# Second products of a fused convolution and SoLU layer taken one tile later, with a sixth buffer of transposed p

## The chip, the cores and the metric

One core of a Trainium2 chip runs the whole program. The metric is the device time of one execution in microseconds (us). Three timed runs of the kernel before gave 1180.63, 1186.45 and 1187.74 us, a median of 1186.45. The profiled execution took 1186.25 us by the same clock; its profile spans 1184.5 us from the first to the last instruction, and 1.75 us lie around it.

## The reference

The input x has 8 sequences of 4160 rows and 192 columns. A causal convolution of 7 taps runs along each sequence, with one softmaxed set of taps for each of 8 heads of 24 columns. Its 33280 rows go through a SoLU layer:

```
h    = y @ w_in                                  # 192 -> 1024
e    = exp(h - max(h));  sm = e / (sum(e) + 1e-9)
solu = h * sm
ln   = (solu - mean(solu)) / sqrt(var(solu) + 1e-6) * g_ln
out  = ln @ w_out                                # 1024 -> 192
```

Inputs and outputs are float32 (w_in, w_out and g_ln arrive as 64-bit words). The kernel splits each operand of a matmul into an upper and a lower half of 16 bits and adds three products, which keeps nearly all of float32's precision.

## The kernel before, in words

**Tiles and chunks.** A tile is 128 rows; there are 260. The convolution works on chunks: chunk 0 has 1024 rows, chunk 1 has 1056, and chunks 2 to 16 have 2080 each (16.25 tiles). A chunk's x arrives in four pieces (`Chunk.load`, L141 to L169) into eight buffers `xr`, so that a piece of chunk n+2 takes a buffer of chunk n. The peaks of a piece are taken in eight steps by VectorE (`sum_squares`, L183), a small matmul adds them up (`add_up`), a chain of eight small VectorE operations makes the chunk's scales (`scale_steps`, L194 to L213), and the last link of that chain writes three columns of `cv` on GpSimd (L210). Then GpSimd splits each piece into halves in three operations (`halve_steps`, L243, L247, L250); those are put in a queue with costs, and `queue.run(budget)` issues entries as long as its credit is above zero (L1146). TensorE convolves the halves (`fold`, L1654), ScalarE and VectorE write the result as upper and lower y (L320, L329), and three transposing DMAs for each of a chunk's two parts turn y into yT (`turn`, L359).

**One tile.** TensorE makes ph = y @ w_in in two PSUM banks (`up_half`, L802). VectorE takes the row's extreme (`emit_max`, L853), ScalarE the exponential e (`emit_exp`, L860), VectorE the numerators ph times e (`emit_mul`, L870), ScalarE their upper half (`emit_hi`, L881) and the sum of squares (`emit_square`, L885), and GpSimd the lower half (`emit_lo`, L896). The same call then has SyncE (SP) issue one transposing DMA, which turns both halves, p, into pT (L898). TensorE makes the second product po = pT @ w_out (`out_half`, L932), VectorE moves po to a group's buffer (`emit_evac`, L969), and when a group of 8 tiles has its roots (`Group.roots`, GpSimd, L1027 to L1031), each row block is scaled and stored. Four buffers hold e, four hold p16, five hold pT (tag `pT`, taken in turn), three pairs of PSUM banks hold ph or a convolution, and two single banks hold po.

**The order of the work is written out by hand** (`manual_schedule`): each engine, and SP's queue of DMAs too, executes its instructions in the order in which the functions issue them. Tiles 0 to 31 go in pairs and threes, tiles 32 to 253 in 111 calls of `two_steps(i)` (L1693), the last six in `three_steps(254)` and `last_three`. One call of `two_steps` issues for TensorE: the first products of tiles i and i+1 (a and b) but for half of b's; one half of the second products of two earlier tiles, x = i-5 and z = i-4; the rest of b; the other half of x and z. Two tiles share the array, 64 rows each, so x and z run side by side, and both must be there when the first half begins. With s = (tile of b in its chunk) // 2, steps with odd s have two groups of products of the next chunk's convolution placed within the first half of x and z (`fold`), as long as there is a next chunk; the step with s = 1 also has the small matmul of `add_up`.

GpSimd's order within step i is: lower half of tile i-2 (`emit_lo(pa)`), `queue.run(2.0)`, the scales of `cv` if the chain is there, lower half of tile i-1 (`emit_lo(pb)`), a second `queue.run(2.0)`. SP's order is: stores, a load of x, the transpose of tile i-2, turns of y, the transpose of tile i-1. Second products of a step therefore use a tile whose `emit_lo` was issued late two steps before (i-5) and one whose `emit_lo` was issued early in the step before (i-4).

```
        x, z = tiles[i - 5], tiles[i - 4]
...
        up_half(a, sa, 1)
...
            out_half(x, z, 0)
```

Of the kernel before, what the change touches and what calls it, by code (L numbers as in the profile page):

```python
# [8 lines left out]
F16 = mybir.dt.float16  # L9
F32 = mybir.dt.float32  # L10
# [10 lines left out]
def kernel(  # L21
# [10 lines left out]
    P = 128  # L32
    B, S, D = x.shape
    H, K = weight.shape
# [3 lines left out]
    NFC = F // P  # L38
    NH = F // 512
    HALO = 16  # L40
    CW = P - HALO
    NB = 2 * D // P
    NT = B * S // P
# [25 lines left out]
    cp = ctx.enter_context(tc.tile_pool(name="cp", bufs=1))  # L69
    xp = ctx.enter_context(tc.tile_pool(name="xp", bufs=1))  # L70
    yp = ctx.enter_context(tc.tile_pool(name="yp", bufs=2))
    sp = ctx.enter_context(tc.tile_pool(name="sp", bufs=3))
# [11 lines left out]
    def single(name):  # L84

        nonlocal singles
        singles += 1
        return ps.tile([P, 512], F32, name=name, tag=f"single{singles % 2}")
# [333 lines left out]
        compare_op=ALU.is_equal, fill=0.0, base=0, channel_multiplier=1,  # L422
    )
    NS = CW - TB
    shift = cp.tile([P, NS + P], F16, name="shift")
    pool.memset(shift, 1.0)
    pool.affine_select(
        out=shift, in_=shift, pattern=[[1, NS + P]],
# [130 lines left out]
    valued(halves[0], dve)  # L559


    taps = cp.tile([P, H, CW], F32, name="taps")
    taps_hi = cp.tile([P, H, CW], F16, name="taps_hi")
    taps_lo = cp.tile([P, H, CW], F16, name="taps_lo")
    NQ = CW // TB
# [9 lines left out]
    for e, bank in enumerate(banks):  # L575
        for q in range(2 * per):
            j = q // 2
# [109 lines left out]
        nc.sync.dma_start(wlo[low, 1, :], wlo[top, 1, :])  # L687


    o_inv = cp.tile([P, 1], F32, name="o_inv")  # L690
    t_out = cp.tile([P, 1], F32, name="t_out")
    osq = cp.tile([P, 1], F32, name="osq")
    wof = wo.f.rearrange("p (c d) -> p c d", d=D)
    mean = None
    out_halves = [slice(0, NFC * D // 2), slice(NFC * D // 2, NFC * D)]
# [198 lines left out]

    def emit_lo(t, eng):
        eng.tensor_tensor(t.p16[:, :, 1, :], t.halves, t.p16[:, :, 0, :], ALU.subtract)  # L896
        t.pT = sp.tile([P, 2 * NFC, P], F16, name=f"pT_{t.i}", tag="pT", bufs=5)
        nc.sync.dma_start_transpose(t.pT, t.p16.rearrange("p n a f -> p (n a f)"))  # L898

    def emit_halves(t, eng):  # L900
# [14 lines left out]
    def emit_out(t):  # L915
        t.po = single(f"po_{t.i}")
        t.wide = t.grp.n > 1 and t.i >= PAIRED

        ops, per = [], NFC // NH
        for c in range(NFC):  # L920
            hi = c // per * 2 * per + c % per
            if t.wide:
                ops.append((hi, ohl[:, c].rearrange("p a d -> p (a d)"), 2 * D))
            else:
                ops += [(hi, ohi[:, c], D), (hi, olo[:, c], D)]
            ops.append((hi + per, ohi[:, c], D))
        for j, (a, w, n) in enumerate(ops):
            nc.tensor.matmul(  # L928
                t.po[:, 0:n], t.pT[:, a, :], w, start=j == 0, stop=j == len(ops) - 1
            )  # L930
# [32 lines left out]
    def emit_evac(t):  # L963
        if t.grp.raw is None:
            t.grp.open()
        if not t.wide:
            dve.tensor_copy(t.grp.raw[:, t.g, :], t.po[:, 0:D])
        else:
            dve.tensor_reduce(  # L969
                t.grp.raw[:, t.g, :],  # L970
                t.po[:, 0 : 2 * D].rearrange("p (a d) -> p d a", a=2), AX.X, ALU.add,
            )
        (rows if t.grp.ready else t.grp.waiting).append((t.grp, t.g))
# [88 lines left out]
    tiles, lefts, left = [], [], 0  # L1062
    for ch in range(NCH):
        lefts.append(left)
        n = (left + spans[ch][2]) // P
        for k in range(n):
            t = Tile()
# [93 lines left out]
    queue, groups, chain, rooted, rows, stores = Queue(), {}, [], [], [], []  # L1161
# [31 lines left out]
    def run_stores():  # L1193
        while stores:
            stores.pop(0)()

    def run_chain(n):
        while chain and n > 0 and chain[0][1] is None:
            chain.pop(0)[0]()
            n -= 1  # L1200
# [16 lines left out]
    PAIRED = FIRST // P  # L1217
# [4 lines left out]
    def prepare(i):  # L1222
        t = tiles[i]
        c = chunks[t.ch]
        t.yT, t.y2 = c.yT, c.y2
        t.cv = c.cvm if t.k == 0 else c.cv
        pos, n, t.g = t.slot
        if pos not in groups:
            groups[pos] = Group(pos, n)
        t.grp = groups[pos]  # L1230
        return t
# [156 lines left out]
    def others(ts):  # L1388

        work = {}  # L1390
        for q in ts:
            for what, items in chores(q.ch, q.k, q.n).items():
                work.setdefault(what, []).extend(items)
        return work
# [6 lines left out]
    def span(i):  # L1401

        late = i >= 26
        return i - DEPTH + (not late) + (i in (PAIRED, 26)), i - DEPTH + 3 + (not late)

    def three_steps(i):


        a, b, c = ts = [prepare(i + j) for j in range(3)]
        done = [tiles[j] for j in range(*span(i))]  # L1410
        if i == NT - 6:
            leave_two()
            done[0] = None
        work = others(ts)
        added = work.get("sum", [])
        added = [added[:1], added[1:]]
# [24 lines left out]
        def place(n):  # L1441
            for f in [f for f, m in zip(todo, places) if m == n]:
                got.setdefault(n, []).append(f())
            if n == 2 * start:
                total_up(at(n)[0][0].bank if at(n) else None)
# [50 lines left out]
            turns()  # L1496
        run_stores()
        swap = i in (17,20,23,26,)
        if not swap and done[0]:
            emit_out(done[0])  # L1500

        fresh = i == 2 * FIRST // P - 2
# [8 lines left out]
        rest = emit_a(a, b, c, between, not fresh, fresh, behind_rows)  # L1511
        if not behind_rows:
            emit_rows(b, False, True)
        if done[0]:
            emit_evac(done[0])
        place(1)
        run_rows(i)
        uppers(0)
# [174 lines left out]
    def two_steps(i):  # L1693


        a, b = prepare(i), prepare(i + 1)
        x, z = tiles[i - 5], tiles[i - 4]
        ch, s = b.ch, b.k // 2
        c1, c3 = (chunks[ch + j] if ch + j < NCH else None for j in (1, 3))

        run_stores()
        if c3 and s in (0, 1, 2, 4):
            c3.load((0, 1, 2, 4).index(s))
        evacs = []
        if left_over:
            pa, pb, *evacs = left_over
            emit_exp(pb)
        else:
            emit_out(tiles[i - 6])
            evacs = [tiles[i - 6]]  # L1710
            pa = pb = None
        for d in evacs:
            emit_evac(d)
        if pb:
            emit_mul(pb)

        got, summed = [], False
        sa, sb, sc = ring
        up_half(a, sa, 0)
        up_half(b, sb, 0)  # L1720
        up_half(a, sa, 1)
        if s % 2 and c1:
            j = s - 1
            got, half, bank = fold(c1, c1.groups()[j : j + 2], sc)
            out_half(x, z, 0, slice(0, NFC // 2))
            half(0)
            out_half(x, z, 0, slice(NFC // 2, NFC))
            half(1)
            if chain and chain[0][1] is not None and chain[0][1] <= i + 2:
                add_up(i + 2, bank)  # L1730
                summed = True
            ring[:] = [sa, sc, sb]
        else:
            out_half(x, z, 0)
            ring[:] = [sc, sa, sb]
        up_half(b, sb, 1)
        out_half(x, z, 1)

        def move():
            for f in moves[:1]:  # L1740
                f()
            del moves[:1]

        if pa:
            emit_square(pa)
            emit_hi(pb)
            emit_lo(pa, pool)
        else:
            for q in squares:
                emit_square(q)  # L1750
            squares.clear()
        for k, q in doubles:
            k.double(*q)
        doubles.clear()
        move()
        emit_max(a)
        emit_exp(a)
        queue.run(2.0)
        for _ in range(2 + (len(rows) > 8)):
            if rows:  # L1760
                g, j = rows.pop(0)
                g.row(j, act if j % 2 else dve)
        if not summed:
            run_chain(4)
        if c3 and s:
            for j in ((), (0,), (1,), (2,), (3,), (4,), (5, 6), (7,), ())[s]:
                sum_up(c3, c3.halves(j // 2)[j % 2], i)
        for k, pc, hg in got[:1]:
            k.upper(pc, *hg)
        emit_mul(a)  # L1770
        for k, pc, hg in got[1:]:
            k.upper(pc, *hg)
        for k, pc, hg in got:
            k.lower(pc, *hg)
        if pb:
            emit_square(pb)
            emit_lo(pb, pool)
        move()
        emit_hi(a)
        emit_max(b)  # L1780
        run_chain(4)
        queue.run(2.0)
        if got and s in (3, 7):
            part = c1.parts[s == 7]
            if s == 3:
                c1.open(lefts[c1.ch], chunks[ch])
            moves.extend(
                lambda blk=blk: c1.turn(blk, *part) for blk in (1, 0, 2)
            )
            moves.append(lambda: doubles.append((c1, part)))  # L1790
        take_rooted()
        left_over[:] = [a, b, x, z]

    def leave_two():

        a, b, *done = left_over
        run_stores()
        emit_exp(b)
        for d in done:
            emit_evac(d)  # L1800
        emit_mul(b)
        emit_square(a)
        emit_hi(b)
        emit_lo(a, pool)
        emit_lo(b, pool)
        squares.append(b)
# [61 lines left out]
    for i in range(PAIRED, 4 * PAIRED, 3):  # L1868
        three_steps(i)
# [31 lines left out]
```

## Time and profile before

| | |
|---|---|
| median of three runs | 1186.45 us |
| profiled execution, its own time | 1186.25 us |
| its span, first to last instruction | 1184.5 us |
| TensorE matmul busy, weight loads busy | 1130.1 us (95%), 887.3 us (75%) |
| VectorE, ScalarE, GpSimd busy | 992.2 (84%), 998.7 (84%), 891.9 us (75%) |
| DMA | 227.75 MB, 192 GB/s over the span |
| mean granted TensorE clock | 0.994 of full |

The five engines run side by side, each in its own order. Busy shares are means over the span; a short wait of one engine shows in a view of a single stretch. A matmul's end is modelled, since matmuls overlap in the array, so that a TensorE called busy may still be slower than its best pace. In a row of windows the engines' busy times stand in the order PE (TensorE), PEld (its weight loads), DVE (VectorE), ACT (ScalarE), POOL (GpSimd).

### The profile page before, as it was taken

How to read it: one execution, taken by the hardware profiler on the slowest of the kernel's cores; microseconds unless marked ns; L12 is line 12 of the kernel's file. 1: busy time of each engine (PE TensorE's matmuls, PEld its weight loads, DVE VectorE, ACT ScalarE, POOL GpSimd, SP SyncE). 2: the span in 40 equal slices, each digit the busy share in tenths (PEclk: the TensorE clock that was granted, in tenths of full speed). 3: DMA queues.
4: the chain of work that ended last, by engine and by line, in shares of the span. 5: the costliest groups of instructions: out<-in, count | busy, mean ns of one | idle time of the engine just before them, and what ended most of it. 6: DMA issues, size and time to landing. Idle time of an engine off the chain costs nothing.

```text
span 1184.5 us, 34794 instructions
## 1 busy us (share of the span) xinstructions
PE 1130.1 (95%) x13681; PEld 887.3 (75%) x13681; DVE 992.2 (84%) x2024; ACT 998.7 (84%) x1789; POOL 891.9 (75%) x711
## 2 busy tenths in 40 slices
PE   5999998999999999999999999999899999999998
PEld 3675666887869788787877877787687886888866
DVE  7988896887888888888888888888788888788886
ACT  7888996887878888888888888888788788888895
POOL 2867897967779697787868959688596878855664
PEclk9999999999999999999999999999999999999999
DMA  7999999999999999999999999999999999999998
GB/s 205 192 180 190 205 213 213 182 200 191 187 188 209 200 199 193 204 196 206 204 186 194 194 203 185 202 193 178 203 188 200 184 190 163 184 184 177 179 164 180
DMA packets 727474, 227.75 MB, mean 192 GB/s; under 512 B 651647, under 2 KB 725903, under 8 KB 727311
## 3 DMA queue, kind: packets, MB, share of 16 engines
q1 hardware_dynamic: 727310, 225.53, 103.8%
q8 instruction: 108, 1.77, 0.6%
q14 instruction: 56, 0.45, 0.1%
HBM read 33.00 MB, written 25.56 MB: 49 GB/s over the span
## 4 chain that ended last, share of the span: by engine, by line
PE 33%; issue 17%; POOL 12%; DMA 11%; ACT 11%; DVE 9%; PEld 6%; SPq 1%; DVEq 0%; ACTq 0%; POOLq 0%; PEldq 0%
PE po L800 13%; PE ph L800 11%; DMA pT<-p 10%; POOL p L896 7%; PEld L800 6%; DVE ph L853 5%; PE pc L800 3%; ACT sq L885 3%; PE po L928 2%; PE ph L753 2%; ACT e L860 2%; ACT y L320 2%; ACT p L881 2%; DVE e L870 1%; POOL xs L250 1%
## 5 line engine op out<-in xcount | busy, mean ns | idle before, releaser
L896 POOL TENSOR_TENSOR p<-e,p 128x1024 f16<-128x1024 f32 x257 | 547.4, 2134 | 137.6 <-ACT p L881 135.3
L800 PE MATMUL po<-ohl,pT 64*128 64x384 f16 (+1 forms) x7104 | 520.4, 283 | 26.4 <-DMA pT<-p 24.3
L800 PEld LDWEIGHTS <-pT 64*128 64x128 f16 x7104 | 436.2, 94 | 84.8 <-DMA pT<-p 44.4
L800 PE MATMUL ph<-whi,yT 64*128 64x512 f16 x2664 | 487.0, 377 | 4.6 <-DVE e L870 4.0
L870 DVE SCALAR_TENSOR_TENSOR e<-ph,cv,e 128x1024 f32<-128x1024 f32 x248 | 317.9, 1282 | 109.3 <-ACT e L860 108.9
L860 ACT ACTIVATE e<-ph,sm 128x1024 f32<-128x1024 f32 x260 | 289.4, 1113 | 88.6 <-DVE ph L853 75.8
L800 PEld LDWEIGHTS <-yT 64*128 64x128 f16 x3774 | 277.0, 94 | 110.5 <-DVE e L870 4.3
L853 DVE TENSOR_SCALAR_CACHE_REDUCE ph<-ph,cv 128x1024 f32<-128x1024 f32 x248 | 318.9, 1287 | 10.0 <-PE ph L800 7.3
L800 PE MATMUL ph<-wlo,yT 64*128 64x512 f16 x1110 | 300.7, 377 | 0.0
L881 ACT CAST p<-e 128x1024 f16<-128x1024 f32 x245 | 255.8, 1044 | 45.9 <-DVE e L870 45.6
L885 ACT ACTIVATE sq<-e 128x1024 f32<-128x1024 f32 x260 | 273.2, 1051 | 0.2
L969 DVE TENSOR_REDUCE raw<-po 128x192 f32<-128x384 f32 x247 | 126.9, 551 | 5.9 <-PE po L800 3.7
L250 POOL TENSOR_TENSOR xs<-xr,xs 128x960 f16<-128x960 f32 (+1 forms) x56 | 107.4, 1918 | 1.2
L329 DVE SCALAR_TENSOR_TENSOR y<-pc,y 112x432 f16<-112x432 f32 (+5 forms) x140 | 67.8, 532 | 27.3 <-ACT y L320 26.2
L800 PE MATMUL ph<-wlo,y 64*128 64x512 f16 x222 | 83.7, 377 | 0.0
L928 PE MATMUL po<-ohl,pT 128*128 128x384 f16 (+1 forms) x712 | 80.2, 269 | 3.1 <-DMA pT<-p 1.6
L800 PE MATMUL pc<-xs,taps_hi 64*112 64x240 f16 (+1 forms) x832 | 80.8, 259 | 0.0
L928 PEld LDWEIGHTS <-pT 128*128 128x128 f16 x712 | 61.8, 98 | 22.6 <-issue 4.3
L320 ACT ACTIVATE y<-pc 112x432 f16<-112x432 f32 (+5 forms) x140 | 57.1, 470 | 24.1 <-PE pc L800 20.7
L183 DVE TENSOR_REDUCE xa<-xr 128x1 f32<-128x384 f32 x112 | 67.8, 620 | 6.7 <-DMA xr<-in_x_dram 6.7
L800 PE MATMUL pc<-xs,taps_lo 64*112 64x240 f16 (+1 forms) x416 | 70.5, 259 | 0.0
L800 PEld LDWEIGHTS <-taps_hi 64*112 64x112 f16 x832 | 65.6, 128 | 2.2 <-issue 1.7
(166 smaller groups left out, 993.5 us busy)
## 6 DMA issues: line engine op xcount, KB each, us to landing
out_dram<-raw SPq DMA_DIRECT2D x127, 192.0 KB, 2.8
xr<-in_x_dram SPq DMA_DIRECT2D x41, 480.0 KB, 4.7
xr<-in_x_dram SPq DMA_DIRECT2D x22, 384.0 KB, 4.1
pT<-p SPq DMA_TRANSPOSE x263, 5.0
y<-yT SPq DMA_DIRECT2D x15, 140.0 KB, 3.1
y<-yT SPq DMA_DIRECT2D x15, 126.0 KB, 2.8
yT<-y SPq DMA_TRANSPOSE x102, 3.7
raw_out<-in_moe_w_out_dram SPq DMA_DIRECT2D x1, 1536.0 KB, 12.6
```

The source lines that it names most:

```text
L183: dve.tensor_reduce(self.part[:, col : col + 1], self.raw[j][:, a:z, :], AX.XY, ALU.max, apply_absolute_value=True,)
L250: (2.1 * size + 0.2, lambda: pool.tensor_tensor(xl, r, h, ALU.subtract)),
L320: act.activation(self.at(0, col + e, col + z, a, b), pc[:, :, e:z], AF.Copy, scale=self.scale(),)
L800: nc.tensor.matmul(o, lhs, w, start=start, stop=stop)
L853: dve.tensor_scalar(t.ph, t.ph, t.cv[:, 0:1], None, ALU.mult, ALU.min, accum_out=t.bias)
L860: act.activation(t.e, t.ph, AF.Exp, bias=t.bias, scale=-1.0, accum_out=grp.z[:, g : g + 1])
L870: dve.scalar_tensor_tensor(t.e, t.ph, t.cv[:, 3:4], t.e, ALU.mult, ALU.mult, accum_out=t.grp.s1[:, t.g : t.g + 1],)
L881: act.copy(t.p16[:, :, 0, :], t.halves)
L885: act.activation(junk, t.e, AF.Square, accum_out=t.grp.s2[:, t.g : t.g + 1])
L896: eng.tensor_tensor(t.p16[:, :, 1, :], t.halves, t.p16[:, :, 0, :], ALU.subtract)
L928: nc.tensor.matmul(t.po[:, 0:n], t.pT[:, a, :], w, start=j == 0, stop=j == len(ops) - 1)
L969: dve.tensor_reduce(t.grp.raw[:, t.g, :], t.po[:, 0 : 2 * D].rearrange("p (a d) -> p d a", a=2), AX.X, ALU.add,)
```

## The change

- `two_steps` takes the second products of x = i-6 and z = i-5, one tile later than before. At the first such step (i = 32) the separate second product of tile 26 falls away, and at the end `three_steps(254)` makes that of tile 248, which it left out before.
- A sixth buffer of pT, `sixth`, takes every sixth tile from 37 on; the other five go on in turn. It lies where `taps` and `shift` lay, which serve the convolution of the first chunks and are now views of it. `o_inv`, `t_out` and `osq` become columns of one tile.
- The first of the two places in a step where the chain of a chunk's scales goes on issues three links in place of four, so that the GpSimd link (L210) comes at the second place, behind `emit_lo(pb)`.
- The queue is run three times a step with a budget of 1.3 in place of twice with 2.0; the new place is just behind `emit_lo(pb)`.
- While chunk 3 is under way (steps 32 to 46), chunk 6's four pieces of x are loaded at s = 2, 3, 5, 6 in place of 0, 1, 2, 4, and the eight peaks are taken from s = 3 on in place of s = 1. Later chunks keep their places.

```diff
-    shift = cp.tile([P, NS + P], F16, name="shift")
+    sixth = cp.tile([P, 2 * NFC, P], F16, name="sixth")
+    spare = sixth.rearrange("p a b -> p (a b)")
+    shift = spare[:, 2 * H * CW : 2 * H * CW + NS + P]
...
-    taps = cp.tile([P, H, CW], F32, name="taps")
+    taps = spare[:, 0 : 2 * H * CW].bitcast(F32).rearrange("p (h c) -> p h c", h=H)
...
-        t.pT = sp.tile([P, 2 * NFC, P], F16, name=f"pT_{t.i}", tag="pT", bufs=5)
+        if 4 * PAIRED <= t.i < NT - 6 and (t.i - 4 * PAIRED) % 6 == 5:
+            t.pT = sixth
+        else:
+            t.pT = sp.tile([P, 2 * NFC, P], F16, name=f"pT_{t.i}", tag="pT", bufs=5)
...
             leave_two()
-            done[0] = None
...
-        x, z = tiles[i - 5], tiles[i - 4]
+        x, z = tiles[i - 6], tiles[i - 5]
...
-        if c3 and s in (0, 1, 2, 4):
-            c3.load((0, 1, 2, 4).index(s))
+        first = ch == 3
+        when = (2, 3, 5, 6) if first else (0, 1, 2, 4)
+        if c3 and s in when:
+            c3.load(when.index(s))
...
-            emit_out(tiles[i - 6])
-            evacs = [tiles[i - 6]]
...
-        queue.run(2.0)
+        queue.run(1.3)
...
-            run_chain(4)
-        if c3 and s:
-            for j in ((), (0,), (1,), (2,), (3,), (4,), (5, 6), (7,), ())[s]:
+            run_chain(3)
+        if c3:
+            for j in (
+                ((), (), (), (0, 1), (2,), (3,), (4, 5), (6, 7)) if first
+                else ((), (0,), (1,), (2,), (3,), (4,), (5, 6), (7,), ())
+            )[s]:
...
             emit_lo(pb, pool)
+            queue.run(1.3)
...
         run_chain(4)
-        queue.run(2.0)
+        queue.run(1.3)
```

## Rows read from the trace of the kernel before

**Rows 1.** Page, part 1: busy time (share) and instructions of each engine.
```profile
PE 1130.1 (95%) x13681; PEld 887.3 (75%) x13681; DVE 992.2 (84%) x2024; ACT 998.7 (84%) x1789; POOL 891.9 (75%) x711
```

**Rows 2.** TensorE's timeline around a step's start: start, us, instruction, shape, count.
```profile
508.17 2.17 PE L800 MATMUL po<-ohl,pT 64*128 64x384 f16 x32
510.13 0.43 PE L800 MATMUL ph<-whi,yT 64*128 64x512 f16 x2
```

**Rows 3.** Windows: three quiet steps; stretch, us, busy (instructions), clock, DMA share, GB/s.
```profile
371.63:379.44 7.81, 7.81 (x105) 7.31 (x101) 7.35 (x15) 6.65 (x12) 7.81 (x5) 1.00 0.96 193
379.44:388.35 8.91, 8.91 (x128) 8.41 (x125) 7.82 (x17) 8.03 (x16) 7.14 (x6) 1.00 0.95 174
396.16:405.41 9.25, 9.25 (x129) 7.68 (x125) 8.20 (x16) 8.65 (x16) 6.79 (x7) 1.00 1.10 197
```

**Rows 4.** Windows: steps 32 to 250, and the end of the kernel behind them.
```profile
169.70:1135.95 966.25, 935.25 (x12262) 759.38 (x12263) 808.17 (x1624) 821.57 (x1452) 745.71 (x572) 1.00 1.06 192
1135.95:1184.50 48.55, 42.74 (x379) 29.90 (x374) 36.86 (x94) 34.64 (x63) 25.82 (x26) 1.00 0.93 174
```

**Rows 5.** Groups by line: mean ns of one, idle before; the convolution's products count its steps.
```profile
L800 PE MATMUL pc<-xs,taps_hi 64*112 64x240 f16 (+1 forms) x832 | 80.8, 259 | 0.0
L800 PE MATMUL pc<-xs,taps_lo 64*112 64x240 f16 (+1 forms) x416 | 70.5, 259 | 0.0
L928 PE MATMUL po<-ohl,pT 128*128 128x384 f16 (+1 forms) x712 | 80.2, 269 | 3.1 <-DMA pT<-p 1.6 <-DVE raw L969 1.4
```

**Rows 6.** Waits, whole span: engine, line and releaser, us in total, times, longest.
```profile
POOL cv L210 <- DVE cv L207: 47.5, 14, 6.1
PEld L800 <- DMA pT<-p: 44.4, 46, 3.2
PE po L800 <- DMA pT<-p: 24.3, 25, 2.8
DVE xa L183 <- DMA xr<-in_x_dram: 6.7, 1, 6.7
PE ph L800 <- DVE e L870: 4.0, 1, 4.0
PE po L800 <- DVE ph L853: 1.5, 1, 1.5
PE ph L800 <- DVE xm L205: 0.6, 1, 0.6
ACT e L860 <- POOL xs L250: 1.4, 5, 0.3
```

**Rows 7.** Windows, as in rows 3: steps 98 to 104 (s = 1 to 4) of one chunk.
```profile
464.85:474.10 9.25, 9.25 (x128) 7.16 (x125) 7.96 (x16) 8.49 (x15) 6.78 (x7) 1.00 1.10 191
474.10:481.90 7.80, 7.80 (x104) 5.61 (x102) 7.62 (x21) 6.45 (x12) 4.37 (x5) 1.00 1.26 213
481.90:493.25 11.35, 9.37 (x129) 7.78 (x127) 7.87 (x17) 8.18 (x15) 11.03 (x10) 1.00 1.09 209
493.25:501.06 7.81, 7.81 (x104) 6.64 (x101) 6.96 (x14) 6.80 (x15) 6.65 (x4) 1.00 1.05 207
```

**Rows 8.** GpSimd's timeline in the same chunk (idle before and its releaser in brackets).
```profile
474.45 2.13 POOL L896 TENSOR_TENSOR p<-e,p 128x1024 f16<-128x1024 f32 x1 [2.38 <-ACT p L881]
479.60 0.59 POOL L210 TENSOR_SCALAR cv<-cv 128x1 f32<-128x1 f32 x3 [3.02 <-DVE cv L207]
480.15 2.14 POOL L896 TENSOR_TENSOR p<-e,p 128x1024 f16<-128x1024 f32 x1
```

**Rows 9.** SP's and TensorE's timelines behind it.
```profile
480.93 4.06 SPq L898 DMA_TRANSPOSE pT<-p  x1
487.23 0.58 PE L800 MATMUL po<-ohl,pT 64*128 64x384 f16 x6 [1.98 <-DMA pT<-p]
```

**Rows 10.** Windows, as in rows 3: steps 34 and 36 together, and step 54.
```profile
177.77:201.18 23.41, 18.84 (x228) 13.25 (x226) 15.61 (x36) 14.71 (x25) 16.20 (x16) 0.93 1.02 214
270.50:284.13 13.63, 10.88 (x128) 9.23 (x125) 7.21 (x15) 7.46 (x14) 9.79 (x7) 0.87 1.14 184
```

More of the change, by code (lines that the diff above doesn't have):

```diff
@@ L687, in settle_rest @@
         nc.sync.dma_start(wlo[low, 1, :], wlo[top, 1, :])
-    o_inv = cp.tile([P, 1], F32, name="o_inv")
-    t_out = cp.tile([P, 1], F32, name="t_out")
-    osq = cp.tile([P, 1], F32, name="osq")
+    of_out = cp.tile([P, 3], F32, name="of_out")
+    o_inv, t_out, osq = (of_out[:, j : j + 1] for j in range(3))
     wof = wo.f.rearrange("p (c d) -> p c d", d=D)
@@ L1498, in three_steps @@
         swap = i in (17,20,23,26,)
-        if not swap and done[0]:
+        if not swap:
             emit_out(done[0])
@@ L1513, in three_steps @@
             emit_rows(b, False, True)
-        if done[0]:
-            emit_evac(done[0])
+        emit_evac(done[0])
         place(1)
```

## The prediction

> **What bounds the kernel now.** I began with the page's busy line [rows 1]: TensorE at 95%, the next engine at 84%. To see whether that 95% is work at full pace, I looked for a step's start in TensorE's timeline, where the 32 products of x and z end and the first products of the next pair begin [rows 2], and cut the span at such starts. Quiet steps repeat to a hundredth: 7.81 us without convolution, 8.91 with it, 9.25 at s = 1, where the small matmul of the chunk's scales comes in [rows 3]. TensorE is busy for the whole of each, while VectorE, ScalarE and mostly GpSimd have room. So these are its paces, and no edit takes a product away.
>
> The long middle, steps 32 to 250, is 110 steps in 966.25 us [rows 4]. The convolution's (832 + 416) / 24 = 52 groups of products [rows 5] mark 52 steps, 13 of them with s = 1; 58 have none. At the quiet paces that is 58 x 7.81 + 39 x 8.91 + 13 x 9.25 = 920.7 us. So 45.5 us are lost in the middle. TensorE's idle time there is 966.25 - 935.25 = 31.0 us; the rest is slow running after a wait. Where it goes is in the waits [rows 6]: TensorE's matmuls wait 24.3 us for pT, its weight loads 44.4 us in 46 waits, at most 3.2. The others in the middle are 4.0 + 1.5 + 0.6.
>
> One chunk shows how pT comes late [rows 7]: s = 1 and 2 run at pace, s = 3 takes 11.35, s = 4 is at pace again. GpSimd makes a lower half at 474.45 to 476.58, then stands 3.02 us before the three links of `cv`, waiting for VectorE's part of the chain, and only then does the next lower half, from 480.15 [rows 8]. SP has had the transpose in hand since 480.93, and TensorE resumes at 487.23 after 1.98 us of idling [rows 9]. That wait of GpSimd is there 14 times, 47.5 us in all [rows 6]. In the same stretch GpSimd has most of the split of x to do: it is busy for 11.03 of the 11.35 us [rows 7].
>
> The first chunk has a case of its own: VectorE stands 6.7 us before a peak of x that was not loaded [rows 6]. TensorE then waits 4.0 for a bank, and steps 34 and 36 take 23.41 in place of 9.25 + 7.81 [rows 10].
>
> **The change part by part.** *One tile later.* No instruction is added; what comes first in a step's second products now is a tile whose lower half was issued late two steps before, where until now z's was issued early in the step before. That is half a pair of steps, (7.81 + 8.91) / 4 = 4.2 us more time for each pT. The longest wait for pT is 3.2 us, 2.8 on the matmul [rows 6]. So each wait seen goes as long as GpSimd does not fall further behind when TensorE no longer stops. *The sixth buffer* keeps the distance between a buffer's last read and its next write: tile i-2's transpose now takes the buffer of i-8, read in step i-2, as it took i-7's. Only at the start do tiles 31, 33 and 35 get a buffer whose last product ends with the step, up to 7.8 us later than the first product of that step; pT of these has 4.2 us more, but behind such a wait SP holds stores and loads. That costs between nothing and 6.3 us, the price of the one late load that the trace has [rows 10]; I take nothing, since the loads of just these steps move later too.
>
> *The scales on GpSimd* go behind the second lower half. The 3.02 us of [rows 8] then come before no lower half; by the time GpSimd is there, VectorE's three links are done. Behind them the queue of pieces waits at most as long as now. This alone would have covered the 1.98 of [rows 9].
>
> *Halves in small portions.* The budget is 3 x 1.3 = 3.9 a step in place of 4.0. A chunk's entries cost, by the code's numbers, 3 x 4.73 + 3.9 = 18.1, and two groups of roots 6.0. From s = 2 to 7 the old budgets give 22, the new 20.8: some 3 units go into the next chunk, where only the first two pieces are needed at s = 1. No piece gets forced, and no operation is added: nothing, hidden by GpSimd's free time about the change of chunks (6.78 busy of 9.25 at s = 1, 4.37 of 7.80 at s = 2, [rows 7]). If that cover were gone, a piece would cost its split in front of a lower half, and the 4.2 us would take it.
>
> *First loads later.* The peak at s = 1 of chunk 3's time moves to s = 3, its load to s = 2, so the 6.7 us wait goes. Worth 23.41 - 17.06 = 6.3 us [rows 10], already within the 45.5. VectorE gets two peaks at s = 3, 6 and 7 in one chunk; they lie beside TensorE.
>
> *Tile 26's own second product* goes at the start and tile 248's comes at the end: 80.2 us for 712 matmuls [rows 5] is 1.8 us for 16. The end is mostly TensorE's, 42.74 of 48.55 [rows 4], so +1.8 there and -1.8 before 169.70; net 0, between -1.8 and +1.8. *Shared storage* of `taps`, `shift` and the scalars: the copies of taps read what the products of `shift` left in PSUM, so they stand behind these already; 0.
>
> *The clock.* In the two worst stretches the granted clock averages 0.93 and 0.87 [rows 10], that is, TensorE ran at 1.2 instead of 2.4 GHz for a part of them, after idling 4.0 and 2.8 us [rows 6]. It costs 0.07 x 23.4 + 0.13 x 13.6 = 3.4 us, which comes back with the waits and is within the 45.5.
>
> *Sum.* 1186.25 - 45.5 = 1140.7 if all is won. What stays: VectorE's 1.5 + 0.6 of waits [rows 6], and I allow one short wait a chunk, 13 x 0.3 (the size of the shortest that show, [rows 6] has 0.3 on ScalarE): 6 us. That gives **1147 us**. The profiled execution is 0.2 us under the median of the runs shown, so the sum needs no correction for it; one of the three runs lies 6 us lower.
>
> A rule that bears on the size: the Trainium skill (Perfetto Trace Analysis, Identifying the Most-Contended Engine) holds the matmul's busy share to be a poor measure of how close TensorE is to its limit. By busy share only the 31.0 us idle in the middle could be won, which would give 1155; by the paces, 45.5 and 1141. The trace agrees with the rule: step 36 and step 54 show busy time at half clock that the busy share counts as work.
>
> **The rivals.**
>
> *A: the 16 DMA engines become the bound.* DMA shares are 1.05 to 1.26 [rows 7], and TensorE's stops have given transposes time. Steps s = 1 to 4 move 9.25 x 191 + 7.80 x 213 + 11.35 x 209 + 7.81 x 207 = 7417 KB; without the stall they must do it in 33.8 us, 219 GB/s, more than any row of a step shows here except 214 [rows 10]. At 213 they need 34.8, 1 us a chunk more: 13 us, 1147 + 13 = 1160. Against it: the rest of a chunk runs at less, 174 to 197 in quiet steps [rows 3], so that a backlog of 1 us can drain there, and it is smaller than the 4.2 us. The skill (Trainium Kernel Development and Optimization, Key Constraints) says that DMAs of all queues run on the same 16 engines and interleave; by that rule a sixth buffer brings no bandwidth, which is this rival.
>
> *B: GpSimd becomes the bound at s = 3.* It was busy 11.03 of 11.35 there [rows 7]. If those 11.03 us must pass before the step can end, each chunk keeps 11.03 - 8.91 = 2.1: 13 x 2.1 = 27, so 1147 + 27 = 1174. The wait would show on ScalarE, before an e or p16 buffer that GpSimd or the transpose has not left. For it: 1.4 us of such waits are there already [rows 6]. Against it: over s = 1 to 4 GpSimd is busy 28.83 of 33.8 us at pace, and the lag lets work of s = 3 slide into s = 4.
>
> *C: the lag only moves the lateness.* If GpSimd's lower halves are late because TensorE's own products were, every engine shifts by 4.2 us and the waits come back: 1186. Against it: after a long wait the next step is at pace at once [rows 7].
>
> *D: slower.* SP is one queue. Should the transposes now wait for the buffer of a tile read later, the load of x behind them comes late, as once before step 36, and VectorE stands before a peak. One such case cost 6.3 us [rows 10]. It decides from 7 cases in 13 chunks on (7 x 6.3 = 44 against the 39 won); in all 13, 1147 + 82 = 1229. Against it: the buffer's distance stays as it was, and the only case so far came with the switch from threes to pairs.
>
> **How the numbers follow.** Forecast 0.69, A 0.10, B 0.12, C 0.05, D 0.04. The forecast's own range is 1138 to 1156: from all won and 1.8 us of the moved product on top (1140.7 - 1.8) to the 6.3 us of the start and 3 us more of small waits (1147 + 9.3). The range asked, 1138 to 1168, takes in A and the milder half of B and leaves out the rest of B, C and D, some 0.17. About 1% (12 us) is what a measurement of this kernel can tell from no change. Faster by more: forecast, A and nearly half of B, 0.85; within 1%: C and the rest of B, 0.11; slower: D, 0.04.
>
> **What would show it.** Right: weight loads wait for pT under 10 us in all, GpSimd's wait at `cv` nearly gone, VectorE's wait for x gone, clock 1.00 throughout the middle, and its 110 steps in 920 to 930 us with s = 3 near 8.9. Wrong: the s = 3 steps still at 10 or more, with TensorE waiting for VectorE instead of pT and ScalarE for GpSimd (B); pT waits with GpSimd idle and transposes landing later (A); pT waits of the same size (C); VectorE before x once a chunk (D).

## The result and the profile after

Three runs of the changed kernel took 1143.27, 1144.20 and 1144.46 us, median 1144.2 against 1186.45 before: ratio 0.9654, 95% interval 0.9604 to 0.9705. The profiled execution took 1143.27 us, with a span of 1141.6.

The page of the kernel after, part 1, and the bytes moved in 40 slices of 28.5 us (GB/s):

```profile
PE 1119.9 (98%) x13681; PEld 771.7 (68%) x13681; DVE 989.7 (87%) x2024; ACT 996.1 (87%) x1789; POOL 893.1 (78%) x711
...
GB/s 223 194 185 184 216 210 202 205 225 214 226 213 197 218 197 215 194 193 218 198 196 203 202 218 198 203 213 183 220 200 212 216 174 169 183 149 202 189 146 180
```

The counts are those of [rows 1]; nothing was added or taken away. The windows of the kernel after are the stretch ahead of the first step's start, steps 32 to 250, the end, and steps 98 to 104 of the chunk of [rows 7]:

```profile
0.00:165.90 165.90, 151.34 (x1030) 97.97 (x1031) 145.30 (x302) 140.49 (x274) 118.52 (x113) 0.99 0.93 200
165.90:1090.50 924.60, 924.21 (x12261) 642.67 (x12262) 806.08 (x1627) 819.99 (x1452) 748.20 (x573) 1.00 1.03 201
1090.50:1141.60 51.10, 44.39 (x396) 31.06 (x392) 38.34 (x97) 35.63 (x65) 26.34 (x27) 0.98 0.75 169
...
444.23:453.53 9.30, 9.30 (x129) 7.00 (x127) 8.25 (x16) 8.70 (x17) 6.79 (x7) 1.00 0.97 222
453.53:461.34 7.81, 7.81 (x105) 4.62 (x102) 7.63 (x21) 6.46 (x12) 4.97 (x6) 1.00 1.16 199
461.34:470.37 9.03, 9.03 (x128) 5.84 (x126) 7.95 (x17) 8.15 (x15) 8.93 (x6) 1.00 0.88 200
470.37:478.18 7.81, 7.81 (x105) 4.64 (x102) 6.96 (x14) 6.80 (x14) 6.19 (x6) 1.00 1.17 229
```

The middle went from 966.25 [rows 4] to 924.60 us, 41.65 of the 42.9 us by which the span fell. TensorE idles 0.4 us of it. The step with s = 3 takes 9.03 in place of 11.35 [rows 7]. The stretch ahead lost 169.70 - 165.90 = 3.8 us and the end gained 51.10 - 48.55 = 2.55.

The waits of the kernel after (engine, line and releaser, us in total, times, longest):

```profile
POOL cv L210 <- DVE cv L207: 10.4, 2, 6.4
...
PE po L932 <- DVE raw L973: 3.4, 3, 2.0
...
PE po L932 <- DMA pT<-p: 0.7, 1, 0.7
```

No wait of TensorE or of its weight loads for pT is left in `two_steps` (line L801 now), where [rows 6] has 24.3 and 44.4 us, and none of VectorE for x. What the kernel has more is a wait of 2.0 us for the evacuation of a bank at the end, before the second product of tile 248.

### The profile page after: what moved, and what is told of

Read it like the earlier page. It is cut to its first block, busy times and chain, and to the rows that moved or that the text cites. A ratio compares the mean times of both kernels' runs of the same rounds, so it can differ in the third digit from the quotient of the medians.

```text
span 1141.6 us, 34802 instructions
## 1 busy us (share of the span) xinstructions
PE 1119.9 (98%) x13681; PEld 771.7 (68%) x13681; DVE 989.7 (87%) x2024; ACT 996.1 (87%) x1789; POOL 893.1 (78%) x711
## 4 chain that ended last, share of the span: by engine, by line
PE 70%; issue 10%; DVE 10%; ACT 5%; DMA 1%; POOL 1%; SPq 1%; PEld 0%; DVEq 0%; ACTq 0%; POOLq 0%; PEldq 0%
PE po L801 28%; PE ph L801 28%; DVE ph L854 6%; PE pc L801 4%; PE po L932 4%; PE ph L754 3%; ACT e L861 2%; DVE e L871 2%; ACT sq L886 1%; PE pc L288 1%; PE ph L783 1%; DMA raw_in<-in_moe_w_in_dram 1%; POOL p L897 1%; DVE y L329 1%; PEld L801 0%
## 5 line engine op out<-in xcount | busy, mean ns | idle before, releaser
L801 PE MATMUL po<-ohl,pT 64*128 64x384 f16 (+1 forms) x5952 | 483.7, 283 | 0.0
L801 PE MATMUL ph<-whi,yT 64*128 64x512 f16 x2664 | 450.6, 376 | 0.0
L801 PEld LDWEIGHTS <-pT 64*128 64x128 f16 x5952 | 347.2, 94 | 93.5
L801 PEld LDWEIGHTS <-yT 64*128 64x128 f16 x3774 | 219.4, 94 | 163.0 <-DVE xm L205 2.6
L801 PE MATMUL ph<-wlo,yT 64*128 64x512 f16 x1110 | 261.5, 376 | 0.0
L801 PE MATMUL po<-ohl,sixth 64*128 64x384 f16 (+1 forms) x1152 | 155.5, 283 | 0.0
L801 PEld LDWEIGHTS <-sixth 64*128 64x128 f16 x1152 | 102.7, 94 | 18.2
L801 PE MATMUL ph<-wlo,y 64*128 64x512 f16 x222 | 83.5, 376 | 0.1
L932 PE MATMUL po<-ohl,pT 128*128 128x192 f16 (+1 forms) x696 | 78.4, 268 | 4.5 <-DVE raw L973 3.4
L801 PE MATMUL pc<-xs,taps_hi 64*112 64x240 f16 (+1 forms) x832 | 70.2, 258 | 0.3 <-DVE e L871 0.2
L754 PE MATMUL ph<-whi,yT 128*128 128x512 f16 x216 | 58.3, 380 | 1.5 <-DVE e L871 1.5
```

The costliest lines, as they stand in the source:

```text
L754: nc.tensor.matmul(bank, lhs, w[:, r, n * 512 : (n + 1) * 512], start=start and j == 0, stop=stop and j == len(ops) - 1,)
L801: nc.tensor.matmul(o, lhs, w, start=start, stop=stop)
L932: nc.tensor.matmul(t.po[:, 0:n], t.pT[:, a, :], w, start=j == 0, stop=j == len(ops) - 1)
```

## The experiments

Theory L says that the lag covers each late pT, whatever makes it late; theory G that GpSimd's order had to be mended. Each kernel was timed in turns with the kernel before. The first four shared a chip (before: 1183.58 us), the next four another job (before: 1182.76), the last four a third (before: 1182.13).

**The lag alone** (`lag_alone`): the kernel after, with the other parts set back.

```diff
-            run_chain(3)
+            run_chain(4)
...
-        first = ch == 3
+        first = False
...
-        queue.run(1.3)          # three places
+        queue.run(2.0)          # two places
```

> The kernel after with only the later second products, the sixth buffer and the shared storage kept: scales, portions of x and first loads are as in the kernel before. Theory L (the 4.2 us of more time cover every wait for pT whatever makes it late): no wait of TensorE for pT is left; what stays against 1144 is the first chunk's late x, 6.3 us, so 1150 to 1152 us, and VectorE waits 6 to 7 us for x once. Theory G (it was GpSimd's order that had to be mended): the wait at cv stays, and with it 13 waits of 1 to 2 us, so 1162 to 1175 us.

Measured 1147.88 us, ratio 0.9712 (0.9674 to 0.9750). Its waits:

```profile
POOL cv L210 <- DVE cv L207: 40.1, 13, 4.0
...
DVE xa L183 <- DMA xr<-in_x_dram: 3.9, 1, 3.9
```

GpSimd waits before `cv` nearly as it did, and TensorE never waits for pT in `two_steps`. L's mechanism holds; the time is 2 us under its range, because the late x cost less than the 6.3 us I took from [rows 10] (VectorE waits 3.9 us, where I expected 6 to 7).

**All but the lag** (`rest_no_lag`):

```diff
-        x, z = tiles[i - 6], tiles[i - 5]
+        x, z = tiles[i - 5], tiles[i - 4]
...
-            t.pT = sixth                       # every sixth tile
+            t.pT = sp.tile(..., tag="pT", bufs=5)
```

> The kernel after with the second products back at tiles i-5 and i-4 and five buffers; the later scales, the small portions and the later first loads are kept. Theory L: most waits for pT come back, less the 14 waits of GpSimd at cv: in the trace after, pT of tile i-4 lands behind the start of the second products by at most 4.7, 4.5, 1.1, 0.3, 0.1, 1.0, 1.4, 1.3, 2.9, 4.3, 2.8, 0.8 and 0.1 us in its 13 chunks, 25 us in all, so 1160 to 1172 us. Theory G: no more than 6 us above 1144, so 1144 to 1150 us.

(The separate second product of tile 26 is back too, and that of tile 248 is left out again.) Measured 1161.97 us, ratio 0.9829 (0.9788 to 0.9871), so faster than the kernel before by 1.3 to 2.1%, and at the near end of L's range. The waits for pT are back at half their size before:

```profile
PEld L801 <- DMA pT<-p: 20.1, 16, 3.7
...
PE po L801 <- DMA pT<-p: 11.0, 8, 3.3
```

So either part alone wins much of the same time, 36 us with the lag and 22 without it; they overlap. Theory G, which gave all but 6 us to the order of GpSimd, falls.

**Five buffers** (`lag_five`): the sixth buffer is not used.

```diff
-        if 4 * PAIRED <= t.i < NT - 6 and (t.i - 4 * PAIRED) % 6 == 5:
-            t.pT = sixth
-        else:
-            t.pT = sp.tile(..., tag="pT", bufs=5)
+        t.pT = sp.tile(..., tag="pT", bufs=5)
```

> The kernel after with five buffers of pT and no sixth. The transpose of tile i-1 in step i then needs the buffer of tile i-6, which the second products read until the end of the same step, and SP holds its stores and loads behind it. Theory L (what counts is the distance of lower half and product; there is slack of 1 to 9 us per transpose): some waits of TensorE for pT, 1146 to 1160 us. Rival D (SP held by buffers makes loads of x late): VectorE waits for x or TensorE for yT in each chunk, 1180 to 1230 us.

Measured 1143.74 us, ratio 0.9677 (0.9637 to 0.9718). No range held: this is the time of the kernel after, under L's 1146, and far from D's. SP now does wait for TensorE to leave a buffer:

```profile
SPq L899 <- PE po L801: 72.1, 33, 4.5
```

That is up to 4.5 us at a time, and it costs nothing that can be measured; VectorE does not wait for x. With the other parts in place the gain does not need the sixth buffer.

**The scales early again, with the lag** (`cv_early`): `run_chain(3)` back to `run_chain(4)`.

> The kernel after with four links of the chain at the first place again, so that GpSimd's three links of cv stand in front of the second lower half. Theory L: GpSimd waits there again 3 us a chunk, but the slack of the second products (mostly 3 to 9 us at s = 4, 0.9 in one chunk) takes nearly all of it: 1144 to 1149 us. Theory G: the waits for pT come back, 13 times 1 to 2 us, 1157 to 1170 us.

Measured 1144.70 us, ratio 0.9680 (0.9648 to 0.9712). GpSimd waits before `cv` again, 43.6 us in 13 waits, and the time does not show it. L holds.

**The old portions, with the lag** (`old_portions`): two runs of the queue at 2.0. Beside it ran the kernel after once more (`after_again`).

> The kernel after, unchanged, as the mark for the three kernels beside it on this chip: 1143 to 1146 us.

> The kernel after with two runs of the queue at 2.0 in place of three at 1.3. Theory L (the lag covers what GpSimd's order costs): within 2 us of the kernel after. Rival G: larger pieces stand in front of the second lower half and the waits for pT come back in the middle of each chunk, 10 to 20 us more.

Measured 1144.62 us for the kernel after (0.9685, 0.9660 to 0.9711) and 1144.19 for the old portions (0.9675, 0.9649 to 0.9701): the same.

**The old first loads, with the lag** (`old_loads`): `first = False`.

> The kernel after with chunk 6's loads and peaks in their old places. Theory L: VectorE waits for x once, 4 to 7 us, and TensorE loses 3 to 6 us behind it, with nothing else changed: 1147 to 1150 us. Rival: the wait was a matter of when SP came to the load, the lag has moved that, and the time is that of the kernel after within 1 us.

Measured 1146.81 us (1146.52 to 1148.13), 2.2 over the kernel after beside it; ratio 0.9702 (0.9678 to 0.9726), so the intervals overlap. The profile places it: steps 34 to 46 take 2.8 us more than in the kernel after, and the rest of the middle takes the same (table below). VectorE waited for x once, 3.6 us. The sign is as expected; the sizes lie at or under the low end of what I expected.

**The end** (`tail_swap`): the second product of tile 248 behind the first products of tile 254.

```diff
-        swap = i in (17,20,23,26,)
+        swap = i in (17,20,23,26,NT - 6,)
```

> The kernel after with the second product of tile 248 issued behind the first products of tile 254 in place of before them. TensorE stood 2.0 us there for the evacuation of a bank by VectorE. Theory: that wait is filled, 1.0 to 2.0 us less than the kernel after. Rival: the end is set by the last tiles' own chain, and the time is the same within 0.5 us.

Measured 1141.91 us (1140.19 to 1142.48), ratio 0.9656 (0.9632 to 0.9680): 2.7 under the kernel after beside it, and the lowest median here, though the intervals of the ratios overlap. Its windows put 2.06 us of that in the end, against 924.60 and 51.10 above:

```profile
167.15:1091.76 924.61, 924.12 (x12262) 643.82 (x12263) 806.14 (x1627) 819.95 (x1452) 748.20 (x573) 1.00 1.03 201
1091.76:1140.80 49.04, 44.30 (x396) 31.23 (x392) 38.29 (x97) 35.53 (x65) 26.32 (x27) 1.00 0.81 176
```

The 2.0 us wait for a bank is gone from this trace.

**The scales alone** (`cv_alone`): the kernel before with `run_chain(3)` at the first place and nothing else.

> The kernel before with one edit: three links of the chain at the first place of a step, so that GpSimd's links of cv come behind the second lower half. Theory O (the wait at cv is what made pT late at s = 2 and 3): the 47.5 us of waits at cv go and about half of the waits for pT with them, 1163 to 1172 us. Rival: GpSimd is busy with pieces of x there anyway, the lower half comes no earlier, and the time stays within 5 us of the kernel before.

Measured 1183.67 us against 1182.13, ratio 0.9994 (0.9964 to 1.0024). Theory O falls:

```profile
PEld L800 <- DMA pT<-p: 39.1, 40, 2.9
PE po L800 <- DMA pT<-p: 21.1, 20, 2.5
POOL cv L210 <- DVE cv L207: 10.4, 2, 6.4
```

The wait at `cv` shrinks from 47.5 to 10.4 us as it does in the kernel after, and TensorE waits for pT almost as before. The rival's time is right, but its reason is not: in the chunk of [rows 8] the second lower half does come earlier, at 478.74 in place of 480.15, while SP takes up its transpose at 485.39 in place of 485.74. The rows of GpSimd and SP in that chunk:

```profile
478.74 2.13 POOL L896 TENSOR_TENSOR p<-e,p 128x1024 f16<-128x1024 f32 x1 [2.23 <-ACT p L881]
...
485.39 2.89 SPq L898 DMA_TRANSPOSE pT<-p  x1
```

**More work for GpSimd** (`lo_half_more`, `lo_twice`): the second lower half is computed once more, by half (shown) or in whole, in front of itself.

```diff
+            pool.tensor_tensor(pb.p16[:, :1, 1, :], pb.halves[:, :1], pb.p16[:, :1, 0, :], ALU.subtract)
             emit_lo(pb, pool)
```

> The kernel after with half of the second lower half of each step computed once more in front of it (1.07 us of GpSimd, 111 times, 119 us in all; the values are the same). Theory L: TensorE sets the pace and the smallest slacks of pT are 0.9 and 1.6 us, so waits come in the first two chunks alone: 1144 to 1150 us. Rival B (GpSimd is the next bound, 78% busy): waits in every chunk, 1155 us or more.

> The kernel after with the second lower half of each step computed twice (2.13 us of GpSimd, 111 times, 237 us; GpSimd would then be busy 1130 of 1144 us). Theory L: this is past the cushion; GpSimd falls behind at s = 3 to 6 in each chunk by more than the slack, waits for pT return, 1165 to 1200 us. Rival: the slack of 4 to 9 us holds this too in most chunks, 1146 to 1160 us.

Measured 1148.89 us (ratio 0.9718, 0.9690 to 0.9746) with 1.07 us more a step, and 1224.31 (1.0350, 1.0319 to 1.0381) with 2.13 us. The first is within L's range. The second is past even the range expected for being past the cushion. The busy line of its page, its waits, and the window of its middle:

```profile
PE 1136.9 (93%) x13681; PEld 878.1 (72%) x13681; DVE 991.4 (81%) x2024; ACT 997.7 (82%) x1789; POOL 1123.1 (92%) x821
...
ACT p L882 <- DMA pT<-p: 60.0, 44, 4.3
...
PE po L801 <- DMA pT<-p: 34.4, 29, 3.0
...
168.00:1171.00 1003.00, 943.00 (x12261) 751.43 (x12259) 807.50 (x1624) 820.83 (x1452) 973.05 (x681) 0.99 0.90 185
```

GpSimd is busy for 973 of the 1003 us, more than any other engine, and the wait of rival B shows: ScalarE stands before a p16 buffer whose transpose is not through. VectorE also waits for x, 26.5 us in 12 waits.

**Stores twice** (`store_twice`): each group's store is issued a second time.

```diff
         def store(self, a, z):
             ...
+            nc.sync.dma_start(out[...], self.raw[:, a:z, :])
```

> The kernel after with each group's store issued twice (25 MB more to HBM, 253 MB in all; the same values go to the same places). Theory L: the DMA engines have room, the transposes land a little later and the slack takes it: 1144 to 1150 us. Rival A (the DMA engines are next to binding at 200 GB/s): time goes up with the bytes once the slack is gone, at the 213 GB/s of the busiest step before 253 MB take 1189 us.

Measured 1325.71 us, ratio 1.1214 (1.1180 to 1.1248), far past both. It does not test the bytes as I meant it to: the second store goes to the same rows, and SP holds it until the first has landed.

```profile
SPq L1057 <- DMA out_dram<-raw: 258.7, 128, 3.8
...
ACT p L882 <- DMA pT<-p: 128.4, 56, 9.0
...
PE po L801 <- DMA pT<-p: 62.3, 34, 5.4
...
DVE xa L183 <- DMA xr<-in_x_dram: 19.1, 9, 4.8
```

SP stands 258.7 us in 128 waits with every transpose queued behind, and only 191 GB/s are moved, less than the 200 of the kernel after. With SP held some 2 us about once a step, the kernel takes 181 us more; what the added bytes cost by themselves is not told apart from that.

**The middle of each profile.** Windows cut at the starts of steps 34, 48 and 252, one profile of each kernel, us (the loads of the change differ in the first stretch alone):

| | steps 34 to 46 | steps 48 to 250 |
|---|---|---|
| before | 66.89 | 891.29 |
| after | 59.99 | 856.29 |
| `lag_alone` | 63.47 | 856.33 |
| `old_loads` | 62.78 | 856.33 |
| `rest_no_lag` | 62.23 | 872.35 |
| `cv_alone` | 68.92 | 887.07 |

Behind step 48 the lag alone takes all that the whole change takes, 35.0 us. Runs of the kernel before differ by up to 13 us (1178.33 to 1191.73 in the third job), so a few us against its row say little.

## Why the prediction was right, and where it was not

**The paces, and the lag.** The sum of quiet steps, 920.7 us for the middle, was the right measure: it took 924.6, 3.9 over, where I had allowed 6. The time of 1147 was 2.8 us above the median and 3.7 above the profiled execution, whose windows hold 3.35 of it: 2.1 in the middle and 2.0 at the start (3.8 where I had 1.8), less 0.75 at the end (2.55 where I had 1.8). The 2.0 at the start have no cause that I can show; the same code took 167.15 us there in `tail_swap`, so that 1.25 of them are within what executions differ by. The lag covered every wait seen, at most 3.2 us [rows 6], and `lag_alone` shows that it does so without the other parts. The 4.2 us are a mean, and not for each pT: an odd tile is used in the same step as before, an even one a whole step later. What counts is that a step's last pT is now that of tile i-5, and in the kernel before, that had landed at least 1.6 us before the step's second products began, in each of the 101 steps for which the trace has its landing.

**The clock** of the kernel after is 1.00 over steps 34 and 36 together, and over step 54. In the kernel before it was 0.93 and 0.87 there [rows 10], after TensorE had idled 4.0 and 2.8 us; those waits are gone. The price of 3.4 us was not measured by itself.

**The busy share** would have given 1155 and the paces 1141, or 1147 with the waits that I let stay; measured is 1144.2. This agrees with the Trainium skill (Perfetto Trace Analysis, Identifying the Most-Contended Engine), which holds the matmul's busy share to be a poor measure of how close TensorE is to its limit.

**What made pT late** I read wrongly. The step that failed is the one from [rows 8] to [rows 9]: that the lower half of 480.15 is the one for which TensorE waited until 487.23, so that moving `cv` "alone would have covered the 1.98". `cv_alone` gained nothing. Transposes and lower halves both come once a tile and in the order of tiles, so they can be counted off. SP's timeline of the kernel before in that stretch:

```profile
470.78 0.46 SPq L162 DMA_DIRECT2D xr<-in_x_dram  x1
471.35 3.60 SPq L898 DMA_TRANSPOSE pT<-p  x1
475.00 1.31 SPq L359 DMA_TRANSPOSE yT<-y  x1
476.42 3.27 SPq L898 DMA_TRANSPOSE pT<-p  x1
479.80 0.52 SPq L1049 DMA_DIRECT2D out_dram<-raw  x1
480.37 0.46 SPq L162 DMA_DIRECT2D xr<-in_x_dram  x1
480.93 4.06 SPq L898 DMA_TRANSPOSE pT<-p  x1
485.05 0.58 SPq L372 DMA_DIRECT2D y<-yT  x1
485.74 2.77 SPq L898 DMA_TRANSPOSE pT<-p  x1
```

and GpSimd's, from a little earlier:

```profile
467.85 4.22 POOL L896 TENSOR_TENSOR p<-e,p 128x1024 f16<-128x1024 f32 x2
```

The transposes that start at 471.35, 476.42, 480.93 and 485.74 are those of the lower halves from 467.85 (two), 474.45 and 480.15 [rows 8]. So step 102 waited for the lower half of 474.45, done at 476.58, ahead of `cv`. SP came to it only at 480.93: it runs from one DMA to the next without a gap, and was busy with the transpose before it, a store and a load of x. GpSimd's 3.02 us were off the path. This is no single case: counted off in the same way, in 20 of the 25 waits of TensorE for pT (20.9 of their 24.3 us, [rows 6]) SP took up the transpose 2.5 to 6.4 us after the lower half was done; in the other five it was within 1 us. Whether a change of SP's order alone would cure the kernel before was not tried. The forecast did not suffer, because it took the 45.5 us as a whole, and the lag gives time to the whole way from lower half to product, SP's part too.

**The other parts.** With the lag in place neither the later scales nor the small portions can be measured (`cv_early`, `old_portions`), as I had costed the portions; the gain I gave the scales is not there without it either. The first loads are worth 2 to 3 us with the lag, not 6.3, since the lag alone takes some of those steps' loss (66.89 to 63.47 us). The sixth buffer, which I took to be what keeps SP free, can be left out. The moved product cost more than 1.8 us at the end by a wait for a bank, which `tail_swap` takes away.

**The rivals.** A's limit of 213 GB/s is no limit: a step of the kernel after moves 229 and slices of its page 225 and 226. Where the DMA engines do bind was not tried, since `store_twice` turned out to be a test of SP. B lies near: against the kernel after in other jobs, 1.07 us more a step costs 4 to 5 us, 2.13 costs 80. C falls: no wait for pT is left in `two_steps`. The sign of D, VectorE before x, shows where SP is held at every store (`store_twice`), but a wait for a buffer of pT does not set it off (`lag_five`). By the prediction's own chances, what its range leaves out adds up to 0.15 or 0.16, not 0.17.

**Open:** how the 22 us that `rest_no_lag` has without the lag are made up. Of the 23.6 us that its profile gains from step 34 on, 18.9 lie behind step 48, where its loads of x stand as before; so in these profiles the first loads give at most 4.7. The 18.9 are left to the small portions, alone or together with the later scales; by themselves the scales gain nothing that can be measured (`cv_alone`), and the portions were not run alone. How the portions would do it is not shown; SP's delay behind a lower half, counted off as above over tiles 30 to 249, has a median of 1.9 us in the kernel before, 2.1 in `cv_alone` and 0.2 in `rest_no_lag`.

## What to carry to other kernels

Take the floor from stretches that repeat to a hundredth rather than from a busy share, and price a scheduling change against it. Where a product waits now and then for a long way through several queues, give it more distance before mending any one of them; here that won 36 of 42 us. Before blaming a wait that lies near, count off which instance feeds which through in-order queues: here all but 10.4 us of a wait of 47.5 were removed without an effect that could be measured.

## What was not expected of the hardware

In these traces a transposing DMA issued on SP right behind a load of x (480 KB here) mostly held SP longer than others did. In the kernel after, the rows of the longest such case are these:

```profile
453.36 1.69 SPq L902 DMA_TRANSPOSE sixth<-p  x1
455.15 0.52 SPq L1053 DMA_DIRECT2D out_dram<-raw  x1
455.73 0.51 SPq L162 DMA_DIRECT2D xr<-in_x_dram  x1
456.34 6.00 SPq L902 DMA_TRANSPOSE pT<-p  x1
```

Its lower half was done at 456.13; SP was held until 462.34, and the load landed at 462.46. In the kernel before, two such transposes ended at 474.95 and 484.99, and the loads ahead of them landed at 475.21 and 485.22. In the middle of the kernel before, 43 transposes of pT behind a load (480 or 384 KB) took a median of 3.6 us of SP, the 178 others 2.5; in the kernel after 3.5 (44) and 1.8 (176). At the same place in a step, that of an even tile, it is 3.6 behind a load and 2.6 behind a store before, 3.5 and 1.7 after. This is what the traces show side by side; that the load is the cause was not tried.
